# Two blocks of the hidden dimension in the opening, rows prepared one tile ahead, and a fixed place for last-stage work in a fused FFT and MLP training kernel

## The chip, the cores and the metric

The kernel runs on one core of one Trainium2 chip. The metric is the device time of one execution in microseconds (us), the median over several executions.

Engine names in the profile lines: PE is the matrix engine (TensorE), PEld its weight loads, DVE is VectorE, ACT is ScalarE, POOL is GpSimd, SP is the engine whose queue issues the loads. L502 is line 502 of that kernel's source; line numbers differ by a few lines between kernels, so go by the tile names.

## The reference, cut to what matters

```python
x = A_x                                            # [1, 2048, 1024] bf16, F = 3584
g = sigmoid((x * gate_w).sum(-1, keepdims=True))
a = irfft2(rfft2(x) * (w_r + 1j * w_i))            # spectral branch
h = x @ w1 + b1;  r = max(h, 0)             # the MLP takes x too, B_x is not used
b = (r * r) @ w2 + b2                              # MLP branch, squared relu
out = g * a + (1 - g) * b
# returned: out, and the gradients by vjp of A_x, w_r, w_i, w1, b1, w2, b2, gate_w
```

The work on the matrix engine falls into stages. **Opening**: transposes of x and of the gated output gradient db, the first transform stage of x, and the first of the 14 blocks of the hidden dimension F. **Blocks**: the other hidden products and the products for the hidden gradient, beside the first transform stage of the gradient. **Weight gradients** (tiles `pw`), beside the middle transform stages. **Last passes**: the output (`acc`), then the input gradient (`accg`), the former beside the end of the last transform stage (`pki`, `pui`).

## The kernel before

Only the parts that the change touches. Every `yield` is a point where the driver may put another stage's work.

```python
def turned(dst, k, tile_, block, eng):        # transposes into PSUM tile pt, copied out by eng
    for hh in range(2):
        pt = tps.tile([P, DC // 2, 2, P], BF16, name="pt", tag="tr", bufs=2)
        ...                                   # 8 transposes
        eng(out=dst[...], in_=pt[...])        # x: ScalarE -> xT; gradient: VectorE -> dbT

def hidden(fc, ss, w1g, h2T):                 # 8 products ph, then ScalarE: rT = relu, h2T = square
def grads(fc, sb, ss, rT, dhT):               # 8 products pd, then VectorE: dhT = 2 * pd * rT

def mlp_in():                                 # the blocks of F, one after the other
    for fp in range(FC // 2):
        ...
        for sp in range(2):
            for sh in range(2):
                ...
                if fp == 0:
                    rT = [hidden(c, ss, w1g, h2T[:, c, hs]) for c in range(2)]
                    yield
                ...
                for c in range(2):
                    if fp > 0:
                        rT = {c: hidden(2 * fp + c, ss, w1g, h2T[:, c, hs])}
                    last = grads(2 * fp + c, sb, ss, rT[c], dhT[:, c, hs])
                    ...
                    if fp > 0 or c == 1:
                        yield
```

The last transform stage keeps no fixed place. A scheduler orders each engine's instructions:

```python
def folded(n):                                # VectorE: rf from r, needed by half of pki
    V(out=fold[n][:, 0], in0=a, in1=b, op=ALU.add)
    V(out=fold[n][:, 1], in0=a, in1=b, op=ALU.subtract)
def rows_back(n):                             # PE: 8 products pki, 4 from r and 4 from rf; ScalarE: rt
def columns_back(n):                          # PE: 8 products pui from rt; ScalarE: e; VectorE: ev, tt, yo
    ...
for n in range(len(tiles) + 1):
    if n < len(tiles):
        rows_back(n)
        yield
    if n > 0:
        columns_back(n - 1)
    ...
    if n + 1 < len(tiles):
        folded(n + 1)
    yield
```

In the output pass each tile of 128 rows loads and prepares its rows at its own head:

```python
for t2 in range(BW // P):
    t = k * (BW // P) + t2
    a_ = ...; ld(out=a_[:], in_=ax_scr[0][t][:])
    go = ...; ld(out=go[:], in_=go_perm[t])
    af = wb.tile([P, D], FP32, name="af", tag="af", bufs=1)
    STT(out=af[:], in0=a_[:], ...)            # the three of VectorE's "preparation"
    nc.vector.tensor_tensor_reduce(...)       #   sum of af * go
    STT(out=af[:], in0=af[:], ...)
    for hf in range(NH):
        acc = mps.tile([P, H], FP32, name="acc", tag="acc", bufs=4)
        for fc in range(FC):                  # a "unit": 28 products
            mm(acc[:], lhsT=cur[:, fc, t2::2], rhs=w2[:, fc, cs], ...)
        last = STT(out=ot[:, cs], in0=acc[:], ..., in1=af[:, cs], ...)       # the "eviction"
        nc.vector.tensor_tensor_reduce(..., in0=acc[:], in1=go[:, cs], accum_out=bGo[...])
        yield 6
```

And the driver of the opening, one round for each four tiles of rows:

```python
for i0 in range(0, NT, 4):
    ...
    gate(i0); next(stage, None); next(units); next(stage, None)
    for k in (i0 // 2, i0 // 2 + 1):
        turned(dbT, k, lambda i: dbn[:, i, :], of_tile, nc.vector.tensor_copy)
        next(stage, None)
    if i0 + 4 < NT:
        for k in (i0 // 2 + 2, i0 // 2 + 3):
            x_pair(k)
            next(stage, None)
    next(units); next(stage, None); next(stage, None)
for _ in stage:                               # the whole first stage of x lies in the opening
    pass
first = first_stage_of_grad()
mixed = spread(units, first, 0.55)            # 0.55 steps of the side stage to a unit
while n < 78: ...
```

## Time and profile before

| | before |
|---|---|
| time, median of 3 | 1335.81 us (1335.26 to 1336.68) |
| profiled span | 1334.6 us |
| span start to first `pw` product (opening and blocks) | 466.45 us |
| first `pw` to first `acc` (weight gradients) | 454.73 us |
| first `acc` to first `accg` (output pass) | 213.54 us |
| first `accg` to the end | 199.88 us |

These four stretches add up to the span. They are read from the timeline of the matrix engine, as the start of the first product of each kind.

The profile's lines of this kernel are in the prediction.

### The profile page before, as it was taken

To read this page: it belongs to the slowest core of one execution; us is meant where nothing else is said; L and a number is where in the kernel's file an instruction comes from. 1 tells how busy PE (TensorE), PEld (TensorE's weight loads), DVE (VectorE), ACT (ScalarE), POOL (GpSimd) and SP (SyncE) were. 2 spreads that over 40 slices of the span, in tenths; PEclk is the share of its full clock that TensorE was granted. 3 is DMA by queue.
4 is the path that set the end of the run, shared out by engine and by line. 5 is a ranking of instruction groups with operands and counts; after the bars stand their busy time and mean duration, and the time that the engine had idled before them with its cause. 6 is when DMAs were issued, how large, how long until landed. Compare 5 with 4: busy or idle time off the path is not lost.

```text
span 1334.6 us, 18965 instructions
## 1 busy us (share of the span) xinstructions
PE 1298.0 (97%) x6974; PEld 630.2 (47%) x7082; DVE 836.0 (63%) x1669; ACT 424.5 (32%) x722; POOL 295.7 (22%) x484
## 2 busy tenths in 40 slices
PE   7889999999999999999999999999999899999998
PEld 4644444444444444444444445555444444444443
DVE  6986777676666596785667863434756776842232
ACT  6863555555433323232332323443111111000000
POOL 0222232232222253533442212121000000000000
PEclk9999999999999999999999999999999999999999
DMA  7547787788768988889886557778888854663530
GB/s 274 188 161 242 242 254 255 236 259 247 242 207 241 278 252 186 215 201 218 215 174 180 145 156 231 234 251 250 207 223 218 246 163 136 206 180 97 147 103 24
DMA packets 217094, 273.06 MB, mean 205 GB/s; under 512 B 16988, under 2 KB 152170, under 8 KB 217002
## 3 DMA queue, kind: packets, MB, share of 16 engines
q1 hardware_dynamic: 181306, 153.58, 43.4%
q0 software_dynamic: 35696, 118.27, 27.3%
q8 instruction: 55, 0.90, 0.3%
q14 instruction: 37, 0.30, 0.1%
HBM read 146.99 MB, written 118.51 MB: 199 GB/s over the span
## 4 chain that ended last, share of the span: by engine, by line
PE 83%; DVE 9%; DMA 3%; issue 2%; ACT 1%; POOL 1%; SPq 0%; DVEq 0%; ACTq 0%; POOLq 0%
PE accg L983 14%; PE acc L941 14%; PE pw L875 14%; PE ph L654 13%; PE pd L664 13%; PE pw L858 7%; DMA out_dram<-wo 2%; DVE dbacc L835 1%; PE pui L283 1%; DVE dbT L579 1%; PE pki L504 1%; PE pk L250 1%; DVE x L332 1%; PE pu L283 1%; DVE t L451 1%
## 5 line engine op out<-in xcount | busy, mean ns | idle before, releaser
L654 PE MATMUL ph<-xT,w1g 128*128 128x512 bf16 x869 | 215.6, 382 | 2.1 <-DMA w1g<-in_B_w_dram 0.7
L664 PE MATMUL pd<-dbT,w2T 128*128 128x512 bf16 x876 | 211.5, 381 | 3.9 <-DVE dhT L668 1.8
L875 PE MATMUL pw<-grd,res 128*128 128x512 bf16 x896 | 202.4, 379 | 0.0
L858 PE MATMUL pw<-dbn,grp 128*128 128x512 bf16 x875 | 199.9, 379 | 1.2 <-issue 0.2
L941 PE MATMUL acc<-w,hblk 128*128 128x512 bf16 x874 | 196.4, 379 | 3.0 <-DVE bGo L943 1.8
L983 PE MATMUL accg<-w1Tr,hblk 128*128 128x512 bf16 x878 | 192.9, 379 | 0.9
L664 PEld LDWEIGHTS <-w2T 128*128 128x128 bf16 x896 | 87.6, 98 | 107.8 <-issue 5.6
L983 PEld LDWEIGHTS <-hblk 128*128 128x128 bf16 x896 | 87.5, 98 | 105.8 <-issue 0.9
L858 PEld LDWEIGHTS <-grp 128*128 128x128 bf16 x896 | 86.8, 98 | 103.1 <-issue 0.9
L941 PEld LDWEIGHTS <-hblk 128*128 128x128 bf16 x896 | 86.6, 98 | 100.5 <-issue 1.9
L875 PEld LDWEIGHTS <-res 128*128 128x128 bf16 x896 | 86.0, 98 | 98.7 <-issue 0.7
L654 PEld LDWEIGHTS <-w1g 128*128 128x128 bf16 x896 | 86.1, 98 | 97.9 <-issue 2.1
L656 ACT ACTIVATE rT<-ph,b1col 128x512 bf16<-128x512 f32 x112 | 77.0, 687 | 142.6 <-PE ph L654 135.6
L668 DVE SCALAR_TENSOR_TENSOR dhT<-pd,rT 128x512 bf16<-128x512 f32 x112 | 75.1, 671 | 55.4 <-PE pd L664 46.0
L988 DVE TENSOR_TENSOR gxo<-accg,g 128x512 bf16<-128x512 f32 x32 | 22.1, 691 | 106.3 <-PE accg L983 100.7
L773 DVE STREAM_TRANSPOSE stg<-h2T 128x512 int32<-128x512 int32 x56 | 39.8, 711 | 64.4 <-ACT h2T L657 64.4
L862 ACT CAST wo<-pw 128x512 bf16<-128x512 f32 x56 | 32.7, 585 | 143.4 <-PE pw L858 127.5
L870 POOL DMA_DIRECT2D out_dram<-wo x112 | 56.0, 506 | 93.2 <-ACT wo L862 76.1
L880 ACT CAST wo<-pw 128x512 bf16<-128x512 f32 x56 | 32.8, 585 | 132.0 <-PE pw L875 103.0
L657 ACT ACTIVATE h2T<-rT 128x512 bf16<-128x512 bf16 x112 | 70.5, 630 | 3.1
L780 DVE STREAM_TRANSPOSE stgd<-dhT 128x1024 bf16<-128x1024 bf16 x56 | 69.3, 1240 | 1.2
L332 DVE TENSOR_TENSOR x<-px,common 128x1024 f16<-128x1024 f32 x32 | 38.8, 1220 | 45.3 <-ACT common L329 45.3
(182 smaller groups left out, 1488.8 us busy)
## 6 DMA issues: line engine op xcount, KB each, us to landing
h2T_scr<-h2T POOLq DMA_DIRECT2D x28, 512.0 KB, 4.6
h_scr<-stg POOLq DMA_DIRECT2D x28, 512.0 KB, 6.9
dhT_scr<-dhT POOLq DMA_DIRECT2D x28, 512.0 KB, 7.4
dh_scr<-stgd POOLq DMA_DIRECT2D x28, 512.0 KB, 7.1
grp<-h_scr SPq DMA_DIRECT2D x112, 128.0 KB
grd<-dh_scr SPq DMA_DIRECT2D x112, 128.0 KB
hblk<-h2T_scr SPq DMA_DIRECT2D x8, 1792.0 KB
hblk<-dhT_scr SPq DMA_DIRECT2D x8, 1792.0 KB
```

What stands on the lines that cost most here:

```text
L332: V(out=x[:, j, :, 0:H].rearrange("p c (i g) -> p c i g", g=4), in0=px[:].rearrange("p c (g i) -> p c i g", g=4), in1=common[:].rearrange( ...
L654: mm(ph[:], lhsT=w1g[:, dc, fc % 2 * P : (fc % 2 + 1) * P], rhs=xT[:, dc, ss], start=(dc == 0), stop=(dc == DC - 1))
L656: nc.scalar.activation(rT[:], ph[:], ACT.Relu, bias=b1col[:, fc : fc + 1])
L657: nc.scalar.activation(h2T, rT[:], ACT.Square)
L664: mm(pd[:], lhsT=w_[:, ec // 2, ec % 2 :: 2], rhs=dbT[:, ec, ss], start=(ec == 0), stop=(ec == DC - 1),)
L668: return STT(out=dhT, in0=pd[:], scalar=2.0, in1=rT[:], op0=ALU.mult, op1=ALU.mult, accum_out=gb1part[:, fc, sb : sb + 1],)
L780: nc.vector.transpose(out=stg[:, :, :, c, :].rearrange("p b k i -> p k b i"), in_=dhT[:, c, :].rearrange("p (k b i) -> p k b i", b=4, i=32),)
L858: mm(pw[:], lhsT=cur[:, t // 2, 2 * fb_ * P + t % 2 : 2 * (fb_ + 1) * P : 2], rhs=dbn[:, t, hf * H : (hf + 1) * H], start=(t == 0), stop=( ...
L870: st(out=dst[q], in_=wo[32 * q : 32 * (q + 1), :])
L875: mm(pw[:], lhsT=xr[t][:, d_ * P : (d_ + 1) * P], rhs=cur[:, t], start=(t == 0), stop=(t == NT - 1),)
L941: mm(acc[:], lhsT=cur[:, fc, t2::2], rhs=w2[:, fc, cs], start=(fc == 0), stop=(fc == FC - 1))
L983: mm(acc[:], lhsT=cur[:, fc, t2::2], rhs=w1T[:, fc, 2 * hf : 2 * hf + 2, :], start=(fc == 0), stop=(fc == FC - 1),)
```

## The change

The intent has three parts. More products in the opening: half of a second block of F joins the first, and part of the first stage of x moves out of the opening to the later blocks. Rows' preparation one tile ahead, so that an eviction never waits for a load. And `pki`, `pui`, `rf` and `ev` tied behind the unit of products before them, in the order of each engine only, not as a wait (`NoSync`). Two loads move with it: that of `gate_w` goes from the head of the output pass to the next pass, and one group of w2 loads comes three steps sooner.

```diff
+    turn = {"PE": None, "DVE": None}
+
+    def in_turn(ins, eng):
+        after(ins, turn[eng], mybir.DependencyClass.NoSync)
...
-            V(out=fold[n][:, 0], in0=a, in1=b, op=ALU.add)
-            V(out=fold[n][:, 1], in0=a, in1=b, op=ALU.subtract)
+            in_turn(V(out=fold[n][:, 0], in0=a, in1=b, op=ALU.add), "DVE")
+            in_turn(V(out=fold[n][:, 1], in0=a, in1=b, op=ALU.subtract), "DVE")
...   (so too the products of pki, the first of pui, and the four instructions of ev)
-        for fp in range(FC // 2):
-            w1g = wb.tile([P, DC, PW], BF16, name="w1g", tag="w1g", bufs=2)
...   (the block loop is split into load_w1, forth = hidden, back_ = grads, finish = stores)
+        both = lambda what, fp, s: [what(fp, s, c) for c in range(2)]
+        load_w1(0)
+        turns = [turn_w2(0), turn_w2(1)]
+        yield
+        for s in range(4):
+            both(forth, 0, s)
+            yield
+            for t_ in turns:
+                t_()
             turns = []
...
+            if s == 1:
+                load_w1(1)
+                turns = [turn_w2(2), turn_w2(3)]
+            if s >= 2:
+                both(forth, 1, s - 2)
+            both(back_, 0, s)
+            if s >= 2:
+                both(back_, 1, s - 2)
+            yield
...   (output pass)
+        def prepare(t, a_, go, earlier=None):
+            ...
+            af = afs[t] = wb.tile([P, D], FP32, name="af", tag="af", bufs=2)
+            first_ = STT(out=af[:], in0=a_[:], scalar=YS, in1=b2_bc[:], op0=ALU.mult, op1=ALU.subtract)
+            after(first_, earlier, mybir.DependencyClass.NoSync)
...
+        prepare(0, *loads(0))
...
+                if t + 1 < NT:
+                    fresh = loads(t + 1)
+                af, go = afs.pop(t), gos.pop(t)
...
-                        mm(acc[:], lhsT=cur[:, fc, t2::2], rhs=w2[:, fc, cs], ...)
+                        turn["PE"] = mm(acc[:], lhsT=cur[:, fc, t2::2], rhs=w2[:, fc, cs], ...)
...
+                    turn["DVE"] = last
+                    if hf == 0 and t + 1 < NT:
+                        prepare(t + 1, *fresh, last)
...   (the input-gradient pass likewise, with prepare_x)
-        next(stage, None)
-    for _ in stage:
-        pass
...
-    first = first_stage_of_grad()
+    def firsts():
+        yield from stage
+        yield from first_stage_of_grad()
+
+    first = firsts()
...
-    mixed = spread(units, first, 0.55)
-    while n < 78:
+    mixed = spread(units, first, 0.62)
+    while n < 75:
```

## The prediction

> **What bounds the kernel now.** The page comes first, to name the engine.
>
> ```profile
> span 1334.6 us, 18965 instructions
> PE 1298.0 (97%) x6974; PEld 630.2 (47%) x7082; DVE 836.0 (63%) x1669; ACT 424.5 (32%) x722; POOL 295.7 (22%) x484
> PE   7889999999999999999999999999999899999998
> DVE  6986777676666596785667863434756776842232
> ```
>
> PE is the bound: 1334.6 - 1298.0 = 36.6 us of idle in the whole span. The diff adds and removes no matrix product (the built order has the same 14152 PE rows as before), so only idle and slow clock can be won. A gain of 2% would be 26.7 us, three quarters of all idle. The two digits under 9 at the left of the PE strip and the 8s near slice 31 say where to look. The stretch table (PE, PEld, DVE, ACT, POOL busy us, then clock) gives the amounts:
>
> ```profile
> 0.00:50.00 50.00, 38.78 (x413) 27.38 (x418) 37.86 (x98) 35.43 (x72) 5.55 (x12) 1.00 0.78 264
> 50.00:100.00 50.00, 43.01 (x424) 27.32 (x427) 43.54 (x102) 34.62 (x72) 11.05 (x17) 0.97 0.45 151
> ...
> 600.00:650.00 50.00, 47.13 (x222) 21.27 (x226) 29.61 (x42) 13.80 (x22) 21.91 (x39) 1.00 0.91 207
> ...
> 1000.00:1050.00 50.00, 47.00 (x261) 23.53 (x264) 33.01 (x91) 8.83 (x14) 4.15 (x8) 1.00 0.79 203
> 1050.00:1100.00 50.00, 48.16 (x254) 23.55 (x258) 40.93 (x99) 6.16 (x9) 3.95 (x8) 1.00 0.68 216
> ```
>
> Idle: 11.2 + 7.0 us in the opening, 3.0 + 1.8 in the third-last 100 us, 2.9 at 600-650, 3.5 in the last 34 us. What PE waited for:
>
> ```profile
> PE pt L578 <- DVE dbT L579: 7.6, 9, 1.8
> PE pt L578 <- DMA src<-in_A_x_dram: 4.1, 1, 4.1
> PE pxs L327 <- DVE sums L320: 2.9, 2, 2.5
> PE pd L664 <- DVE dhT L668: 1.8, 2, 1.5
> PE acc L941 <- DVE bGo L943: 1.8, 1, 1.8
> ```
>
> In the opening the transposes of the gradient (pt) wait for VectorE to empty two PSUM tiles (dbT copies, 1.2 us each). VectorE is full there: in the six stretches of ten us from 30 to 90 us it is busy 10.0, 9.1, 10.0, 10.0, 9.9 and 8.9 us. In the last passes the PE timeline shows two short clusters:
>
> ```profile
> 1038.34 0.38 PE L504 MATMUL pki<-ki,r 128*128 128x128 f16 x4
> 1039.70 0.68 PE L283 MATMUL pui<-ci,rt 128*128 128x256 f16 x8 [0.98 <-ACT e L514]
> 1042.18 6.20 PE L941 MATMUL acc<-w,hblk 128*128 128x512 bf16 x27 [1.80 <-DVE bGo L943]
> ...
> 1056.65 0.38 PE L504 MATMUL pki<-ki,r 128*128 128x128 f16 x4 [1.04 <-ACT e L514]
> 1057.58 0.28 PE L283 MATMUL pui<-ci,rt 128*128 128x256 f16 x1 [0.54 <-ACT rt L506]
> ```
>
> Two rounds of last-stage work (pki, pui) stand back to back there, so each waits for ScalarE to empty PSUM for the other; the products (acc) behind them stand still too.
>
> **What the Trainium skill says.** "PSUM — Partial Sum Buffer", section "Engine vs sequencer instructions": ScalarE and VectorE queues are strict FIFO, and matmuls start and complete in program order. The trace agrees: at 1039-1042 us acc waits behind pki and pui. So the built order tells what can fill a gap. "TensorE: Matmul & The Clock Gate", section "What's actually happening": an idle window of about 3.4 us halves the clock. The trace agrees: after 78-80 us, where PE is busy 0.42 of 2 us, the granted clock is 0.56, 0.50, 0.50, 0.74 in the four us from 81; 1.7 us are lost that no idle column shows. "Perfetto Trace Analysis", section "Optimization Strategy", advises interleaving regimes with different bounds; the opening with more products is that.
>
> **The change, part by part.**
>
> Opening. Before, one F block (64 hidden and 64 pd products) runs beside the transposes; now half of a second block (32 + 32 products) joins in its second half. A product passes every 0.2155 us (8 in 1.72 us in the timeline), so 13.8 us of product work moves in. Six steps of the first transform stage, three tiles of 16 small products (about 1.1 us each), move out to later, where VectorE is busy 35 of 50 us. VectorE loses 3 x 1.5 us of folds and gains four dhT (0.68 each) and one block half's turns (2 x 0.71 + 2 x 1.24): about +2 us. The first 456 PE rows, to about 33 us, are the same in both orders, so the 9.6 us lost there (4.1 us of it the first load) stay. From 33 to 102 us the trace has 7.9 us of idle, 1.7 us of slow clock, and some 1.4 us in which PE counts as busy while its pipeline drains before nine waits (0.16 us each: 0.379 per product against 0.2155): 11 us to be had at most.
>
> I walked the new order by hand with durations from the trace (transposes of 8 0.45 us, dbT copy 1.14, ScalarE copy 1.1, dhT 0.68). For each transpose set: PE is there after the set before it and what the order puts between; the PSUM tile is free when VectorE has done all that its order puts ahead of that copy, plus 1.14; the later of the two counts. An example, the fourth round: PE ends the first 16 transposes at 81.1; pk, one product and two pu follow, to 81.9; VectorE reaches the first copy at 80.7 and ends at 81.85, so the next set starts at 82.0. Then pu and three products last to 83.5, the second copy ends at 83.4, and nothing waits. By round: second round of dbT, waits 1.0 us (1.3 before, drains not counted). Third: the order has only single hidden products between the transposes, and gradient and x transposes stand together (8, 26 and 6), so about 3.2 us against 1.8. Fourth: 4 products and pk, pu lie between, about 0.1 against 2.7, and the slow clock after it goes. New: four hidden tiles are made before the first pd, with three rT buffers and two PSUM buffers, so the second pd waits for dhT and then for ScalarE: 0.4 and 1.0 us in two places. The walk puts the end of the 73.6 us of work (all of block 0 and half of block 1) at 95.3 us; before, the same amount is done at 102.1 us (67.6 us of work at 94.4, then steady). That is -6.8 us. The walk is kind, it has no late DMA and no semaphore delay; I take off 2.3: **-4.5 us**.
>
> Last passes. The order now has exactly one pki or pui set between any two product units (28 products, 6.04 us). All four waits above should go: 0.98 + 1.80 + 1.04 + 0.54 = **-4.4 us**. Rows prepared one tile ahead (1.22 + 1.23 + 1.28 us of VectorE per tile) take their loads from the path of the eviction; VectorE work is unchanged, about 11 of 13 us per tile, and four acc buffers leave three units of slack. I allow +0.3 us for a new wait.
>
> Unchanged: the start, the 2.9 us at 600-650 (PE order in the middle is the same row for row), the 3.5 us at the end. Sum: -4.5 - 4.4 + 0.3 = -8.6 us, 1335.8 to **1327.2 us**.
>
> **Rivals.**
> - A new wait on a store. h2T and dhT have two buffers; with two blocks in turn, the dhT half of block 0 written until about 92 us is wanted again at about 99. Its store is one of several of 512 KB (7.4 us to landing, in the page's list of issues), behind them in POOL's queue. For: in the trace a store already held VectorE 4.4 us at 94-98 us (u waits for z_scr) and cost PE 1.5. Against: stores before were not late otherwise. It would cost 1 to 5 us: 1329 to 1332.
> - The transposes stay the bound. In the third round PE would be busy about 40% for 6 us, and the clock could halve there instead (1.7 us). Opening gain then 1 to 2 us: 1330 to 1331.
> - VectorE sets the pace of the opening, and more products only wait for it. For: of the 62 us that my walk takes from 33 us on it works some 58, PE some 53 (73.6 less about 21 done before), so any slip of VectorE is a slip of the opening. Against: the folds can come later, the copies and dhT are a third of its work, and the order moved three tiles of folds out. If so, dhT is late at every unit and half of the opening's gain or all of it goes: 1330 to 1332.
> - All is filled: -11 and -4.9: 1320.
>
> **Range and chances.** 1321.5 to 1333.5 holds the first two rivals and nearly the full win. Faster by over 2% needs 1309.1, beyond the 11 + 4.9 us that the change touches: 0.01. Slower by over 2% needs 26.7 us of new waits in an order that moves no work: 0.01. Within 2%: 0.98.
>
> **What will show it.** Right: no PE wait over 0.5 us between 1000 and 1100 us (idle there 4.8 to under 0.8); pt waits for dbT 7.6 to about 5 to 6 us, mostly in the third round (55 to 62 us); no halved clock near 80 us; idle of the first 100 us 18.2 to about 13 or 14. Wrong: pd or ph waiting for dhT or rT near 90 to 105 us, VectorE idle there on a dhT_scr or z_scr store, a clock under 1.00 at 58 to 65 us, or new PE waits on rf, pki or bGo in the last passes.

## More of the kernel before

In the timeline of VectorE at the head of the output pass, the columns are start, duration, engine, line, operation, output and inputs, and in brackets the idle time before it and what ended it:

```profile
927.54 0.43 DVE L496 TENSOR_TENSOR rf<-r 128x256 f16<-128x256 f16 x1 [3.47 <-PE pki L504]
...
932.54 1.23 DVE L929 SCALAR_TENSOR_TENSOR af<-a__9562,b_bc 128x1024 f32<-128x1024 f16 x1 [4.23 <-DMA a__9562<-ax_scr]
```

The first preparation (`af`) starts late, at 932.54 us, since VectorE stood 4.23 us waiting for a load, although the first `acc` product began at 921.18 us. But `rf`, which the matrix engine needs for a later `pki`, was made just ahead of that stop, at 927.54 to 928.31 us.

## The result

The changed kernel took **1329.35 us** in the median of 4 runs (1327.80 to 1331.12), against 1335.53 us for the kernel before (4 runs, 1333.90 to 1336.68). The ratio is 0.9955, with a 95% interval of 0.9935 to 0.9975: a gain of about half a per cent, within 2%. (Ratios are the mean time of one kernel's fast runs over that of the other's in the same rounds, so they are not quite the ratio of the medians quoted.)

The changed kernel's four runs lie in two pairs: 1327.80 and 1327.87 us, both at a mean granted clock of 1.000, and 1330.83 and 1331.12 us at 0.998 and 0.997. The profiled execution is the one of 1330.83. The median lies between the pairs, so no execution took it.

The head of the page after, with the strips of 40 slices of the span:

```profile
span 1328.0 us, 19058 instructions
PE 1303.0 (98%) x7082; PEld 629.8 (47%) x7082; DVE 835.7 (63%) x1669; ACT 424.2 (32%) x722; POOL 295.6 (22%) x484
PE   7899999999999999999999999999999999999998
```

A digit 8 at the left has become a 9, and the two 8s near slice 31 are gone. Idle of PE is 25.0 us, against 36.6 before, but the span fell by only 6.6. Look at the counts: 7082 matrix instructions here, 6974 before, beside 7082 weight loads in both. So 108 records were missing before, some of their time was counted as idle, and the idle of the kernel before was overstated. The stretches rest on start times and have this fault only where a first record is missing. That is so for the first `acc` of before, e5 and e7: it starts 0.32 us after the last `pki` ahead of it, where e1, e3 and e10, with the same order there, show 0.11. In those three the passes are 0.21 us longer than printed, and what comes before is as much shorter.

The table of stretches after (columns as in the prediction):

```profile
0.00:50.00 50.00, 38.87 (x424) 27.00 (x425) 37.77 (x94) 35.05 (x70) 5.79 (x12) 1.00 0.78 265
50.00:100.00 50.00, 46.84 (x420) 28.02 (x418) 47.32 (x106) 30.91 (x67) 11.57 (x16) 1.00 0.48 156
...
900.00:950.00 50.00, 47.20 (x257) 23.12 (x256) 28.98 (x79) 10.33 (x16) 5.96 (x12) 0.97 0.68 202
1000.00:1050.00 50.00, 50.00 (x280) 24.79 (x278) 36.28 (x91) 7.29 (x11) 3.80 (x7) 1.00 0.89 232
1050.00:1100.00 50.00, 50.00 (x274) 24.57 (x273) 38.62 (x99) 8.33 (x12) 4.33 (x8) 1.00 0.63 195
```

From 50 to 100 us PE works 3.8 us more and the clock is whole; from 1000 to 1100 us it never stops. But 900 to 950 us has 2.8 us of idle and a clock of 0.97. What PE waited for, in total, times, longest:

```profile
PE pt L584 <- DMA src<-in_A_x_dram: 3.9, 1, 3.9
PE pt L584 <- DVE dbT L585: 3.5, 6, 0.9
PE pt L584 <- ACT xT L585: 2.7, 4, 0.9
PE pki L510 <- DVE rf L502: 2.4, 3, 2.0
PE pxs L333 <- DVE sums L326: 2.2, 2, 1.8
...
PE pki L510 <- DVE rf L503: 0.8, 1, 0.8
```

The wait for `dbT` has halved (7.6 before), and `bGo` and `dhT` are gone from the list. New is `pki` waiting for `rf`. It has its place in the timeline of PE:

```profile
933.47 0.39 PE L510 MATMUL pki<-ki,r 128*128 128x128 f16 x4
935.88 0.23 PE L510 MATMUL pki<-ki,rf 128*128 128x128 f16 x1 [2.02 <-DVE rf L502]
936.89 0.45 PE L510 MATMUL pki<-ki,rf 128*128 128x128 f16 x3 [0.77 <-DVE rf L503]
937.13 7.82 PE L979 MATMUL acc<-w,hblk 128*128 128x512 bf16 x28
```

PE had done the four products from `r` and stood 2.02 + 0.77 = 2.79 us for `rf`. The unit behind took 7.82 us in place of 6.20 us. The reason is in the stretch of the first us of that unit (third number from the right is the clock):

```profile
937.00:938.00 1.00, 1.00 (x6) 0.44 (x5) 1.00 (x5) 0.57 (x1) 0.11 (x1) 0.50 1.23 203
```

The clock is 0.50 in three us and 0.80 in the fourth: 3 x 0.5 + 0.2 = 1.7 us lost. So the place where four waits of 4.36 us were taken away got a new wait of 2.8 us and 1.7 us of slow clock. The stretches of the two profiled runs say the same:

| stretch | before | after | difference |
|---|---|---|---|
| start to first `pw` | 466.45 | 460.66 | -5.79 |
| to first `acc` | 454.73 | 453.72 | -1.01 |
| to first `accg` (output pass) | 213.54 | 213.68 | +0.14 |
| to the end | 199.88 | 199.94 | +0.06 |
| span | 1334.6 | 1328.0 | -6.6 |

With the missing record of before put back (0.21), and the two `pki` products that stand there ahead of its first `acc` (0.11 us), the two middle differences are -0.69 and -0.18. Nearly all of the visible gain is ahead of the output pass, and the output pass, for which half of the gain was predicted, gained next to nothing in this execution.

Why was `rf` late? The timeline of VectorE after:

```profile
924.92 1.23 DVE L953 SCALAR_TENSOR_TENSOR af<-a__9559,b_bc 128x1024 f32<-128x1024 f16 x1 [7.33 <-DMA a__9559<-ax_scr]
...
928.85 0.75 DVE L980 SCALAR_TENSOR_TENSOR ot<-acc,omg,af 128x512 bf16<-128x512 f32 x1
...
930.12 1.22 DVE L953 SCALAR_TENSOR_TENSOR af<-a__9569,b_bc 128x1024 f32<-128x1024 f16 x1
...
931.26 0.75 DVE L980 SCALAR_TENSOR_TENSOR ot<-acc,omg,af 128x512 bf16<-128x512 f32 x1
...
935.41 0.41 DVE L502 TENSOR_TENSOR rf<-r 128x256 f16<-128x256 f16 x1
```

VectorE stands 7.33 us for the first load of the pass. It evicts the first unit at 928.85, though its products began at 914.38 and took 6.20 us. Then come the preparation of the second tile, now ahead of its time (`af` at 930.12), and the second eviction; only then, because it is tied behind that eviction, `rf`. From the first eviction to `rf` it is 6.56 us of unbroken work. Before, the load was as late (the first `af` started 11.4 us after the first `acc` product, here 10.5), but `rf` stood ahead of it. So two causes offer themselves: the late load, or the order that the tie and the early preparation make. The experiments take them apart.

### The profile page after: what moved, and what is told of

Its sections match the earlier page's. It is cut to its first block, busy times and chain, and to the rows that moved or that the text cites. A ratio compares the mean times of both kernels' runs of the same rounds, so it can differ in the third digit from the quotient of the medians.

```text
span 1328.0 us, 19058 instructions
## 1 busy us (share of the span) xinstructions
PE 1303.0 (98%) x7082; PEld 629.8 (47%) x7082; DVE 835.7 (63%) x1669; ACT 424.2 (32%) x722; POOL 295.6 (22%) x484
## 4 chain that ended last, share of the span: by engine, by line
PE 86%; DVE 7%; DMA 3%; ACT 2%; issue 1%; SPq 1%; POOL 0%; DVEq 0%; ACTq 0%; POOLq 0%
PE accg L1039 15%; PE pd L670 14%; PE ph L660 14%; PE pw L902 14%; PE acc L979 13%; PE pw L885 9%; PE pui L289 1%; DMA z<-z_scr 1%; PE pki L510 1%; PE pk L256 1%; PE pu L289 1%; DMA out_dram<-wo 1%; DVE t L457 1%; DVE dbT L585 1%; DVE t L456 1%
## 5 line engine op out<-in xcount | busy, mean ns | idle before, releaser
L660 PE MATMUL ph<-xT,w1g 128*128 128x512 bf16 x896 | 219.2, 381 | 1.0 <-DMA w1g<-in_B_w_dram 1.0
L979 PE MATMUL acc<-w,hblk 128*128 128x512 bf16 x896 | 201.0, 381 | 0.0
```

The lines of the kernel that those rows point to most:

```text
L660: mm(ph[:], lhsT=w1g[:, dc, fc % 2 * P : (fc % 2 + 1) * P], rhs=xT[:, dc, ss], start=(dc == 0), stop=(dc == DC - 1))
L979: turn["PE"] = mm(acc[:], lhsT=cur[:, fc, t2::2], rhs=w2[:, fc, cs], start=(fc == 0), stop=(fc == FC - 1))
```

## The experiments

Ten kernels ran, in three sets, each set with fresh runs of the kernel before on the same chip. All outputs are right. "Passes" is the stretch from first `acc` to first `accg` of the profiled execution, "opening" the one from the start to first `pw`. "Half clock" counts stretches of slow clock, each 3.41 us at half clock, so 1.7 us lost, and in which stage (the start and end of the program, slow in every execution, are left out).

| kernel | median us (runs) | ratio to before [95%] | opening | passes | half clock |
|---|---|---|---|---|---|
| before | 1335.53 (4) | 1 | 466.45 | 213.54 | 1 opening |
| after | 1329.35 (4) | 0.9955 [0.9935, 0.9975] | 460.66 | 213.68 | 1 passes |
| e1_open_only | 1332.18 (6) | 0.9973 [0.9954, 0.9991] | 460.45 | 216.71 | 2 passes |
| e2_last_only | 1334.29 (5) | 0.9983 [0.9971, 0.9995] | 464.44 | 212.17 | 1 opening, 1 middle |
| e3_no_turn | 1331.96 (6) | 0.9966 [0.9952, 0.9980] | 460.08 | 215.20 | 2 middle, 1 passes |
| e4_no_ahead | 1330.41 (5) | 0.9953 [0.9942, 0.9965] | 460.24 | 211.97 | 1 middle |
| e5_turn_late | 1325.05 (6) | 0.9914 [0.9898, 0.9929] | 460.90 | 208.53 | 1 middle |
| e6_early_load | 1326.93 (6) | 0.9921 [0.9906, 0.9937] | 458.34 | 211.72 | 1 middle |
| e7_one_block_moved | 1335.90 (4) | 0.9990 [0.9972, 1.0008] | 464.13 | 213.54 | 1 middle |
| e8_two_blocks_all | 1333.58 (4) | 0.9976 [0.9957, 0.9994] | 462.58 | 215.97 | 2 passes |
| e9_all_early | 1324.35 (4) | 0.9905 [0.9878, 0.9932] | 459.24 | 208.85 | none |
| e10_all_early_turn_late | 1325.57 (4) | 0.9918 [0.9886, 0.9950] | 459.45 | 208.78 | none |

The kernel before had medians of 1336.48, 1337.48 and 1337.33 us in the three sets (11, 11 and 7 runs), so kernels of different sets are compared by their ratios. Where one execution had slow clock and another not, the stretches differ by that much; take it off before comparing.

### One half of the change at a time

**e1_open_only** is the kernel before with the opening's part of the change alone (the block loop and the driver), so it is the changed kernel without these lines:

```diff
-    turn = {"PE": None, "DVE": None}
-    def in_turn(ins, eng): ...              # and its uses in pki, pui, rf, ev
-        def prepare(t, a_, go, earlier=None): ...
-        def prepare_x(t, gx, xo, earlier=None): ...
-                        turn["PE"] = mm(acc[:], ...)
+                        mm(acc[:], ...)
...   (the last two passes as before)
```

> Only the opening is changed; the last passes are as before. Theory A (the opening gives nearly all of the gain, the last passes nothing net): the block-0-and-half-of-1 work is done near 96.5 us as in the changed kernel, the two clusters of waits near 1040-1060 us are back (4.4 us), time about 1329.5 to 1330.5, some 5.5 us under before. Rival (both halves give some, as I predicted -4.5 and -4.4): about 1331.

Measured: 1332.18 us, ratio 0.9973. The opening is as short as in the full change (460.45), and the clusters of the kernel before are all back in the passes. From its list of waits between 900 and 1150 us:

```profile
PE acc L962 <- DVE bGo L964: 1.8, 1, 1.8
PE pki L504 <- ACT e L514: 1.0, 1, 1.0
```

There they even brought two stretches of slow clock (3.4 us lost, from 1035 us on), which the profiled run of the kernel before had not. The time is 1.7 us over what was expected, the place of the waits is as expected.

**e2_last_only** is the kernel before with the other part alone (the tie and the preparation ahead), so it is the changed kernel without these:

```diff
-        both = lambda what, fp, s: [what(fp, s, c) for c in range(2)]
...   (load_w1, forth, back_, finish: the block loop as before)
-    def firsts(): ...
-    mixed = spread(units, first, 0.62)
+    mixed = spread(units, first, 0.55)
...   (the driver as before)
```

> Only the last passes are changed. Theory A: the two clusters are gone (-4.4 us) but the wait of pki for rf behind the third product unit of the first pass (2.8 us) is there too, with or without a halved clock after it (1.6 us), so only 0 to 1.8 us under before, 1333.7 to 1335.5. Rival (the wait on rf belongs to the changed opening's timing): no wait on rf, 4.4 us under before, 1331.

Measured: 1334.29 us, ratio 0.9983. The clusters are gone, and `pki` waits 2.19 + 0.77 us for `rf` at 942 us. So the new wait belongs to the last passes' part and does not need the changed opening; time and wait are as expected. The two parts' gains, 0.27% and 0.17%, add to 0.44%; both together gave 0.45%, each with an interval of 0.1 to 0.2% to either side.

### Which piece of the last passes' part makes the wait

**e3_no_turn**: everything but the tie.

```diff
     def in_turn(ins, eng):
-        after(ins, turn[eng], mybir.DependencyClass.NoSync)
+        return
```

> The changed kernel without the tie of last-stage work to its place; rows still prepared one tile ahead. Theory B (the wait on rf needs the tie: rf must stand behind the first eviction, which waits for the late first load): no wait of pki on rf near 933 us, no halved clock there, no clusters either since the order keeps one set between units: 1325 to 1326.5, 2.8 to 4.4 us under the changed kernel's slower runs. Rival (two preparations in a row are enough to delay rf): the wait stays and the time is the changed kernel's, 1328 to 1331.

Measured: 1331.96 us, ratio 0.9966. The wait at 933 us is gone, but the order is no longer even, and other waits take its place later, which the expectation had ruled out: it missed by 5.5 us (timeline of PE):

```profile
1056.55 1.89 PE L979 MATMUL acc<-w,hblk 128*128 128x512 bf16 x8 [1.40 <-DVE bGo L981]
...
1061.31 0.34 PE L510 MATMUL pki<-ki,rf 128*128 128x128 f16 x3 [2.87 <-DVE rf L503]
```

So the tie removes 4.3 us of waits in this later part of the pass, and it is only at the head that it does harm.

**e4_no_ahead**: the tie stays, each tile prepares its rows at its own head again.

```diff
-        prepare(0, *loads(0))
...
-                if t + 1 < NT:
-                    fresh = loads(t + 1)
+                prepare(t, *loads(t))
...
-                    if hf == 0 and t + 1 < NT:
-                        prepare(t + 1, *fresh, last)
```

(and the same for the second pass, with the buffers of before: `af` 1, `go3` 2).

> The changed kernel with the tie, but every tile's rows prepared at its own turn. Theory B says the wait needs both parts, so without the second preparation in between rf is done about 1.5 us before PE wants it: no wait on rf, no clusters: 1325 to 1327. Rival (the preparation ahead is what clears the clusters): waits of PE on evictions (acc on bGo or ot) near 1000 to 1100 us, 1329 to 1333.

Measured: 1330.41 us, ratio 0.9953, so the same as the full change within its interval. The first load is as late as ever (VectorE stands 7.59 us for it until 926.65 us), and yet the wait at 933 us is gone: without the second preparation in between VectorE gets to `rf` at 933.66 and 934.67, just in time for PE, which comes to these products at 935.15. Some 2.2 us of smaller waits stand at 1047 to 1059 us (0.73 for `bGo`, 0.91, 0.34 and 0.23 for `rf`). Theory B was right about the head (no wait there) and wrong about the rest: the smaller waits are those of the rival, and the time is 3.4 us over the expected range, half of which the profiled run has as a stretch of slow clock in the middle. So preparing ahead, with its larger buffers, is worth these 2.2 us later in the pass, and costs 2.8 us at its head: at the head tie and preparation ahead are each harmless alone. Together, behind a late load, they make the wait.

### The order or the load

**e5_turn_late**: the whole change, but the tie begins only with the evictions of the third tile. The load is as late as ever.

```diff
-                        turn["PE"] = mm(acc[:], ...)
+                        mine = mm(acc[:], ...)
...
-                    turn["DVE"] = last
+                    if t > 1:
+                        turn["DVE"], turn["PE"] = last, mine
```

> The changed kernel, but the tie begins only with the second unit of the third tile, so the folds (rf) of the first units are free of it; the later order is kept. Theory B: the wait of pki on rf near 933 us (2.8 us) and a halved clock behind it are gone and no wait comes near 1040 to 1060 us: acc to accg takes 210.5 to 211 us (213.7 in the changed kernel's profile, 4.4 of it wait and slow clock at 933 to 940), time 1326 to 1328. Rival (the late first load delays the evictions anyway, so PE waits for PSUM instead): acc to accg stays 213 or more, a wait of acc on bGo or ot appears before 960 us.

Measured: 1325.05 us, ratio 0.9914. PE has no wait at all between 900 and 1150 us. VectorE stops for the load as before (timeline of VectorE), but `rf` is done ahead of it:

```profile
923.57 0.42 DVE L503 TENSOR_TENSOR rf<-r 128x256 f16<-128x256 f16 x1
927.76 1.23 DVE L953 SCALAR_TENSOR_TENSOR af<-a__9559,b_bc 128x1024 f32<-128x1024 f16 x1 [3.77 <-DMA a__9559<-ax_scr]
```

The passes take 208.53 us, 5.15 less than in the profiled run of the change: 2.79 of wait, 1.7 of slow clock, and 0.7 that is left over, of which 0.32 is the missing record and the two `pki` products ahead of the first `acc`. Wait, clock and time are as theory B had them, or better (it expected 210.5 to 211 us and 1326 to 1328).

**e6_early_load**: the tie stays, and the row of b2 and the first tile of the spectral output are loaded early, into buffers of their own (to make room, the row of `gate_w` and that of the column sums use other buffers).

```diff
+            if T == 0 and i == 2:                                # in columns_back of tile 2
+                ld(out=later["early"][1][:], in_=ax_scr[0][0][:])
...
-        b2_bc = wb.tile([P, D], BF16, name="b2_bc", tag="bc")
-        ld(out=b2_bc[:], in_=B_b2.partition_broadcast(P))
+        b2_bc, a0 = later["early"]                               # b2 is loaded during the weight gradients
...
-        prepare(0, *loads(0))
+        gos[0] = wb.tile([P, D], BF16, name="go3", tag="go3", bufs=3)
+        ld(out=gos[0][:], in_=go_perm[0])
+        prepare(0, a0, gos[0])
```

> The changed kernel with the bias rows and the first tile's transform rows in buffers that are free long before, so loaded before the first pass begins; tie and order kept. Theory B (the late first load is the cause): VectorE begins the first preparation by 915 to 918 us instead of 925, and PE does not wait for rf near 933 us; acc to accg 210.5 to 211.5 us. Rival (the tie with two preparations in a row costs the wait whatever the load does): the wait of 2 to 3 us stays.

Measured: 1326.93 us, ratio 0.9921; the passes take 211.72 us, and PE still waits 1.75 + 0.78 us for `rf`. At first this looked like proof that the load doesn't matter. The timeline of VectorE tells otherwise:

```profile
917.29 1.22 DVE L954 SCALAR_TENSOR_TENSOR af<-a,b_bc 128x1024 f32<-128x1024 f16 x1
925.57 1.22 DVE L956 CUSTOM_DVE_ANT_0 junk<-af,go 128x1024 bf16<-128x1024 f32 x1 [7.07 <-DMA go<-in_grad_out_dram]
```

The first step of the preparation came early, at 917.29, and the second stood 7.07 us for the one load that I had not moved, the gradient rows `go`. VectorE reached its first eviction at 928.23, 0.6 us earlier than in the changed kernel. The experiment was a miss: it did not do what it was for, so it decides neither for the theory nor for the rival. Its better time can't be put down to the wait, which stayed; in its profiled run there was no slow clock behind the wait, and the opening happened to be short (458.34).

**e9_all_early** mends that: `go` of the first tile is early too (for room, `go3` has two buffers in place of three). Against e6:

```diff
                 ld(out=later["early"][1][:], in_=ax_scr[0][0][:])
+                ld(out=later["early"][2][:], in_=go_perm[0])
...
-        b2_bc, a0 = later["early"]
+        b2_bc, a0, gos0 = later["early"]
...
-        gos[0] = wb.tile([P, D], BF16, name="go3", tag="go3", bufs=3)
-        ld(out=gos[0][:], in_=go_perm[0])
+        gos[0] = gos0
```

> The changed kernel with all three things that the first row preparation needs (the row of b2, the first tile of the spectral output and the first tile of the output gradient) loaded before the pass into buffers of their own; rows' buffer go3 two deep instead of three for room. The run before this one moved only two of the three, and there the first preparation still stopped at 925.6 us for the gradient rows. Theory (late load AND tie together make the wait of the third gap): the first preparation now ends near 921 us, the first eviction follows its products at about 921 to 922 instead of 928.2, rf is done some 5 us before PE asks, so the wait of pki on rf (2.5 to 2.8 us) is gone; first acc product to first accg product 209 to 210 us instead of 211.7, time about 1325. Rival (the tie with two preparations in a row is enough by itself): VectorE has two preparations of 3.7 us and three evictions of 1.4 us before rf whenever the pass starts, so rf stays late and 1.5 us or more of the wait remains; time 1327.

Measured: 1324.35 us, ratio 0.9905, the shortest profile of all (span 1321.6 us). The timeline of VectorE:

```profile
915.95 1.22 DVE L955 SCALAR_TENSOR_TENSOR af<-a,b_bc 128x1024 f32<-128x1024 f16 x1
...
919.85 0.75 DVE L983 SCALAR_TENSOR_TENSOR ot<-acc,omg,af 128x512 bf16<-128x512 f32 x1
...
928.64 0.42 DVE L502 TENSOR_TENSOR rf<-r 128x256 f16<-128x256 f16 x1
```

and that of PE:

```profile
932.15 0.39 PE L510 MATMUL pki<-ki,rf 128*128 128x128 f16 x4
```

The first eviction follows its products (919.85, where they began at 912.83), and `rf` is there in time: its first half starts at 928.64, and PE comes to it at 932.15. No wait, no slow clock, passes of 208.85 us, with the same tie and the same two preparations in a row as in the changed kernel: the rival, that the order alone is enough, falls. So does the other, that the late load alone is enough, by e3, e4 and e5, where it is late and nothing waits at that place. **It takes both**: a load for which VectorE stands 7 us, and an order that puts 6.56 us of its work between the first eviction and `rf`. Each cell rests on few profiles, but they agree: the four executions with both (after, e2, e6 and e8) wait 2.5 to 3.9 us for `rf` there, the five without one of them (e3, e4, e5, e9, e10) not at all.

**e10_all_early_turn_late** has both cures, so its edit is that of e9 and that of e5 together.

> Both cures at once: the three early loads, and the tie that begins only with the third tile. If each cure removes the same wait, the two together are worth no more than one: 1324.5 to 1325.5, no wait on rf and none on bGo in the last passes. If the late load costs something by itself beside that wait, this one is faster than the later tie alone (1325.05) by 0.5 us or more.

Measured: 1325.57 us, ratio 0.9918, passes of 208.78 us. The two cures remove the same wait, and the second adds nothing that can be seen; the time is as expected to within 0.1 us. The ratios of e5, e9 and e10 lie within one another's intervals, so none of them is shown to be the best. All three are clear of the kernel before; e5 and e9 are clear of the changed kernel too, while the interval of e10 still overlaps its (0.9950 against 0.9935).

### The two halves of the opening's part

**e7_one_block_moved** is the kernel before with only the move of stage-x steps out of the opening (rate 0.60). **e8_two_blocks_all** is the changed kernel with the driver of before (all of that stage in the opening, rate 0.55), so with two blocks alone.

```diff
 # e7, against the kernel before
         next(units)
         next(stage, None)
-        next(stage, None)
-    for _ in stage:
-        pass
...
-    first = first_stage_of_grad()
+    first = firsts()                       # the rest of stage x, then the gradient's
-    mixed = spread(units, first, 0.55)
+    mixed = spread(units, first, 0.60)
 # e8, against the changed kernel: the same lines the other way round, with
-    mixed = spread(units, first, 0.62)
+    mixed = spread(units, first, 0.55)
```

> The kernel before, with only the three tiles of the first stage moved out of the opening, one block of products as before. My theory: the gain of the opening (first product of the gradient pass at 460.7 us instead of 466.5) needs the products; moving folds away alone gives under 2 us: 464.5 to 466. Rival (VectorE was the pace, so taking 4.5 us of folds from it is the gain): 461 to 463.

> The changed kernel with two blocks in the opening, but all of the first stage kept in it. My theory: most of the gain stays, first product of the gradient pass at 461 to 463 us. Rival (VectorE is the pace): no gain or little, 464.5 to 466.5.

Measured: 1335.90 (0.9990, not told from 1) and 1333.58 us (0.9976, with the last passes' part in it). The opening takes 464.13 and 462.58 us. The order of the opening in the kernel before ran twice with a profile (before, e2: mean 465.4) and that of the change in eight runs (after, e1, e3 to e6, e9, e10: mean 459.9, from 458.3 to 460.9), so the whole is worth about 5.5 us, moving steps alone some 1.3 and two blocks alone some 2.9. The two executions of the old order both had a stretch of slow clock there, none of the others had, so 1.7 us of each of these numbers may be that. Equal orders differ by 2.0 to 2.6 us between executions and chips, so no finer split is to be had from single profiles; that neither part alone gives the whole is all that I hold for shown. e8 came out as my theory had it (461 to 463); e7 lies between the theory (464.5 to 466) and the rival (461 to 463), so how much VectorE's folds cost is not shown. Without the moved steps there are more waits for PSUM copies in the opening (a transpose of w2 waits 1.9 us for `xT` in e8), without the second block `pd` waits 1.6 us for `dbT` and 1.7 us for `dhT` in e7.

## Why the prediction was right, and where it was wrong

The time, 1329.35 us, lies in the range of 1321.5 to 1333.5, 2.2 us over the predicted 1327.2, and within 2% as forecast. The sum was right partly by chance: the opening and the middle gave more than predicted, and the output pass gave almost nothing of its 4.1 us.

- **PE is the bound, no product is added or removed, so only idle and slow clock can be won**: right. But the 36.6 us of idle was too large, because 108 records were missing; the prediction printed the count 6974 beside 7082 weight loads and did not ask about it. And the slow clock that it counted as to be won depends on more than the order, as shown below.
- **Opening, -4.5 us**: right in mechanism, under-sized. The 73.6 us of work were done at 96.52 us; the hand walk said 95.3, and before it was 102.1. So the walk missed by 1.2 us and the 2.3 us taken off it was too much; the stretches show -5.79, the means over executions about -5.5, and 1.7 of that is the slow clock which both executions of the old order had. The signs came: idle of the first 100 us is 14.3 us (predicted 13 to 14), no slow clock near 80 us, the wait for `dbT` down, to 3.5 us (predicted 5 to 6). The predicted new waits of 0.4 and 1.0 us for `dhT` and ScalarE are not in the list; the waits of transposes for ScalarE's `xT`, not predicted, rose from 1.2 to 2.7 us.
- **The rival of a late store**: it did not come; no wait of that kind stands at 90 to 105 us. **The rival of a slow clock in the third round**: the transposes do wait there (0.16, 0.52, 0.93 and 0.65 us from 58 to 63 us), but the clock stays at 1.00. **The rival of VectorE's pace**: it did not come true for the change as a whole, since the gain came. But with the steps of x kept in the opening (e8) only about half of it came, so that VectorE's load costs nothing there is not shown.
- **Last passes, four waits of 4.36 us go**: right, as e1 against the changed kernel shows; from 1000 to 1100 us PE never stops. Where nothing new comes in (e5, e9, e10) the passes are 4.7 to 5.0 us shorter than before, 4.9 to 5.0 with the missing records put back. One reading was loose: at 1042.18 us `acc` does not stand behind `pki` and `pui` alone. The line names `bGo`, an eviction by VectorE, and that eviction stood in VectorE's queue behind an `ev` for which VectorE waited 6.53 us, until 1039.19. It is VectorE's order that passed the wait on, the same way in which the new wait came about.
- **"I allow +0.3 us for a new wait"**: this is the step that failed. "Four acc buffers leave three units of slack" looked at the evictions, which do have slack (the first comes about 8 us behind its unit, and no `acc` waits for it), and not at what stands behind them in VectorE's queue. `rf` is wanted for the `pki` behind the third unit, at 933.7 us, and could not come before 935.41. The wait measured 2.79 us, and 1.7 us of slow clock followed it in the profiled run: 4.5 us in place of 0.3. The 1.7 us came by chance (next paragraphs), the 2.79 did not. The prediction named the sign ("new PE waits on rf, pki or bGo in the last passes") but gave it no size; the late load that makes it stands in the trace before, 4.23 us of VectorE's idle at 932.54, and was not put beside the new order.

In numbers: opening -5.8 where -4.5 was predicted, output pass -0.2 where -4.1 was (+0.14 as printed). The middle, which the change leaves as it is, gave another -0.7 (-1.0 as printed) in the profiled pair, all of it in one wait that both have (2.47 us before, 1.81 us after, at 615 and 608 us), which no part of the change was meant to touch.

Why does a gap of PE bring slow clock in one execution and not in the next? Its length does not decide: of the gap that all have in the middle, between 604 and 615 us, 2.01 us was enough in e5, and 2.47 us in before was not. The place of the gap decides. In all twelve traces the granted clock changes only at whole multiples of 3.413 us from its first change. Cut each trace into these windows and add up PE's idle time in each (3.41 less the PE busy time of `--windows`):

| largest idle in one window, us | next window at half clock | next window at full clock |
|---|---|---|
| middle, 604 to 615 us | e4 1.98, e5 2.01, e3 2.15, e7 2.28, e6 2.30, e2 2.90 | e9 1.36, e10 1.47, before 1.48, e8 1.54, e1 1.74, after 1.81 |
| output pass | e1 1.98, e3 2.37, after 2.80, e8 3.09 | e4 1.63, e6 1.75, e7 1.85, before 1.86, e2 1.87 (no gap in e5, e9, e10) |

The two columns don't overlap: from 110 to 1310 us, a window with 1.98 us of idle or more (58%) was always followed by half clock, one with 1.87 us or less (55%) never. The gap of 2.47 us in before lay across a border (about 1.0 + 1.5 us), that of 2.01 us in e5 within one window. The windows begin anew in each execution, at 10.3 to 16.3 us, so it is chance where a gap falls: `rf`'s wait of 2.96 us in e2 was split (1.10 + 1.87) and cost no clock, that of 2.79 us in the changed kernel was whole and cost 1.7. A window at half clock that itself had 0.80 to 1.00 us of idle (e1, e3, e8) was followed by a second. In the opening, where transposes stand between the gaps, the border is not clear: 1.84 us was enough in before, 1.90 us was not in e7. This is read from traces; no run sets the place of the windows. The two pairs of the changed kernel's times (1327.8 and 1331 us, clocks of 1.000 and 0.997 to 0.998) fit with none, or one or two, such stretches per execution; the two fast ones have no profile.

## What to carry to other kernels

When an instruction is tied behind another for the sake of an even order, it inherits everything that can make the other late: before tying, look up in the old trace what that queue stops for just there, and add the work that the new order puts in between. The start of a stage is the place to look: here its first loads came behind a large one in their queue, while later in the pass there was slack. To judge a single gap of the matrix engine, ask how its time divides over the clock's windows, and compare executions only after taking the slow stretches off. And an experiment that takes away a late input must take away all of the inputs; check in its timeline that the start really moved before reading its time.

## What the Trainium skill lacked or had wrong

- "TensorE: Matmul & The Clock Gate", section "HAM oscillation — how this bites in real kernels", gives the rule of no PE idle gaps over about 3.4 us. Here less was enough: 1.98 us of idle within one window of 3.41 us was followed by half clock and a loss of 1.7 us, 1.87 us was not (table above). The same page's section "What's actually happening" has the window free-running, and the traces agree: borders at whole multiples of 3.413 us, begun anew in each execution. But it asks for an idle window, and the prediction took the slow clock at 81 us for agreement with that; the window ahead of it, 77.70 to 81.11 us, was idle for 1.84 us only.
- "Perfetto Trace Analysis" does not say that matrix records can be missing from a trace and are then read as idle time: 6974 of 7082 in the kernel before, where idle fell by 11.6 us and the span by 6.6. Comparing the counts of weight loads and products shows it.
- No page that I looked up tells how long a large load holds the next issue on the same queue. In the output pass the issue right behind each load of 1792 KB took 2.2 to 9.3 us in the traces looked at (4.35 us for the row of b2 in the changed kernel, 5.08 us for the first spectral rows in e9); in the input-gradient pass, where it mostly comes 2 us or more later, 0.3 to 6.6 us. The median of all other issues is 0.54 us, with single ones up to 11. In the changed kernel the first load of the pass was issued at 918.91 us, behind these 4.35 us, and used at 924.92: that is part of why it was late, and the rest is its own 6.0 us.
